# Two attentions on one core: the second scores of a turn of six heads go through a copy on VectorE, and ScalarE takes their exponential last

## The chip, the cores and the metric

The kernel runs on one core of a Trainium2 chip. The metric is the device time of one execution in microseconds, as the median of several runs. The engines are named as in the profile: PE (TensorE; its weight loads have the row PEld), DVE (VectorE), ACT (ScalarE), POOL (GpSimd) and SP (SyncE, whose queue issues nearly all DMAs of the part that matters here).

## What is computed

The reference has two attentions over 2048 tokens of width 576, each with 32 heads of 18 columns; their outputs stand side by side. A is plain attention with one key and one value head for all 32 query heads. B has keys and values for each head, works in four segments of 512 tokens, is causal within a segment and mixes in a memory of the segments before.

```python
# A
scores = einsum("bhqd,bkd->bhqk", q, k) * Dh ** -0.5
o = einsum("bhqk,bkd->bhqd", softmax(scores), v)          # then @ wo
# B, for segment s of 4
logits = einsum("bhqd,bhkd->bhqk", qs, ks) * Dh ** -0.5 + mask
a_dot = einsum("bhqk,bhkd->bhqd", softmax(logits), vs)
num, den = phi(qs) @ M, phi(qs) @ z + 1e-6
o = g * num / den + (1 - g) * a_dot                       # then @ wo
M, z = M + phi(ks).T @ vs, z + phi(ks).sum()
```

## The kernel before

The first stage (up to about 330 us) projects queries, keys and values and stores them in HBM. The second stage, in which the change lies, is the attention. Its scores are made transposed: 128 keys on the partitions, 512 queries in the free dimension. A block is four heads of one chunk of 512 queries: 32 blocks of A (4 chunks of 8) with 16 key tiles each, and 32 blocks of B (4 segments of 8) with 3 steps each. The list `after` says behind which A blocks the pairs of B blocks come.

An item is a step of a block with one pair of heads. `scores` makes the two heads of an item with two matmuls (a step of B with two key tiles: four) that run in two halves of the array's rows, into a tile E of two PSUM banks (line 726 for A, 734 for B). ScalarE takes the exponential of the whole tile E into an SBUF tile P (L727, L737); in B, POOL then clears what lies above the diagonal (L741). There are three tiles E (six banks) and nine tiles P. The other two banks are O, in which `products` sums the four heads of a block (L761, columns of 32, so that four heads run side by side), and F, in which the output projection is made in pieces (`out_part`, L648).

The order of PE, ScalarE and VectorE is written out by hand as turns. A turn holds three items, so six heads; where the 32 items of an A block do not divide by three, one turn has two. A turn emits the scores of its three items with their exponentials, then one piece of an output projection if there is one (`run_fill(1)`, four matmuls), then the products of the turn that lies two back. The first item of a turn takes the tile E that the first item of the last turn had, and so on.

```python
for k in range(len(turns) + 2):
    for n, pr in turns[k] if k < len(turns) else []:
        scores(its[n], pr)
    run_fill(1)
    for n, hf in prods[k - 2] if k > 1 else []:
        ...
```

Behind the products of the last blocks of a chunk comes a chain of small steps, put off by turns in the list `later`: VectorE copies O to SBUF (oe, L770) and SP stores it; `sums` loads the softmax sums back (sm), `inverses` takes their reciprocals on VectorE (L609) and stores them; `load_heads` loads the heads (oc) and the reciprocals spread over the columns (rb; in B behind the first segment also the memory's part, nb and another rb); `weigh` multiplies them on VectorE (L634 to L642); then the pieces of the chunk's projection are ready, and each twelfth of it is copied out of F by VectorE (osb, L672) and stored by SP. At most one such step is emitted a turn, and only in turns whose products are A's. The pieces that are left when the scores end are made in a tail, and behind them the projection of the last chunk, which goes into all eight banks.

B's values come from HBM for a whole segment at a time (`load_vseg`, two buffers). `prefetch` loads the stacks of queries and keys one stack (eight heads) ahead.

Of the kernel before, what the change touches and what calls it, by code (L numbers as in the profile page):

```python
# [7 lines left out]
F32 = mybir.dt.float32  # L8
# [3 lines left out]
AF = mybir.ActivationFunctionType  # L12
ALU = mybir.AluOpType
# [5 lines left out]
S, D, H, DH = 2048, 576, 32, 18  # L19
NSEG, L = 4, 512  # L20
C = 512
NCH = S // C
NKT = S // 128
# [3 lines left out]
SCALE = DH ** -0.5  # L27
# [5 lines left out]
KR = 56  # L33
VW = DH + 1
# [3 lines left out]
HALF = (0, 64)  # L38
# [3 lines left out]
BKEYS = [[(0, 0)], [(1, 0)], [(2, 0), (3, 256)]]  # L42
# [17 lines left out]
def attention_pair_kernel(ctx, tc, a_xT, a_w, a_wo, b_xT, b_w, b_wo, b_beta, ident_d, hmask_d, bmask_d, cmask_d, sel_d, zmask_d, selx_d, sely_d, out):  # L60
    nc = tc.nc
# [552 lines left out]

    def load_heads(ab, c, t):
        o_d, r_d = (oA, rA) if ab == "A" else (oB, rB)
        tiles = [pa.tile([128, C], F32, name=n, bufs=4) for n in ("oc", "rb")]
        if ab == "B" and c > 0:
            tiles += [pa.tile([128, C], F32, name=n, bufs=4) for n in ("nb", "rb2")]
        lo, n, R = H0[t], HT[t], RT[t]  # L620
        nc.sync.dma_start(tiles[0][:R], o_d[c][lo : lo + n, 1:VW, :])
        nc.sync.dma_start(tiles[1][:R], r_d[c][lo : lo + n, None, :].to_broadcast([n, DH, C]))
        if ab == "B" and c > 0:
            nc.sync.dma_start(tiles[2][:R], numB[c][DH * lo : DH * lo + R])
            nc.sync.dma_start(tiles[3][:R], rdB[c][lo : lo + n, None, :].to_broadcast([n, DH, C]))
        return tiles

    def weigh(ab, c, t, tiles):

        R = RT[t]  # L630
        o = parts[ab, c][:R, t]
        oc, rb = (x[:R] for x in tiles[:2])
        if ab == "A":
            nc.vector.tensor_tensor(o, oc, rb, op=ALU.mult)  # L634
            return
        if len(tiles) == 2:
            nc.vector.scalar_tensor_tensor(o, oc, omg[:R, t : t + 1], rb, op0=ALU.mult, op1=ALU.mult)
            return
        nc.vector.scalar_tensor_tensor(oc, oc, omg[:R, t : t + 1], rb, op0=ALU.mult, op1=ALU.mult)
        nb, rb2 = (x[:R] for x in tiles[2:])  # L640
        nc.vector.tensor_tensor(nb, nb, rb2, op=ALU.mult)
        nc.vector.tensor_tensor(o, oc, nb, op=ALU.add)  # L642

    def out_part(ab, c, i, t, dst, c0, n, start, stop):

# [69 lines left out]
    def scores(it, pr):  # L715
# [6 lines left out]
        state.setdefault(it, []).append(p)  # L722
        if ab == "A":
            for j, r0 in enumerate(HALF):
                rows = slice(r0, r0 + KR)
                nc.tensor.matmul(e[:, j], kstA[rows, 128 * kt : 128 * kt + 128], st[rows, h, :], start=True, stop=True)  # L726
            nc.scalar.activation(p, e, AF.Exp, scale=SCALE)  # L727
            return
        n = 512 - 128 * kt if kt < 2 else 384
        for k, c0 in BKEYS[kt]:  # L730
            ks = slice(128 * k, 128 * k + 128)
            for j, r0 in enumerate(HALF):
                rows = slice(r0, r0 + KR)
                nc.tensor.matmul(  # L734
                    e[:, j, c0 : c0 + 512 - 128 * k], st[rows, 4 + h, ks], st[rows, h, 128 * k :], start=True, stop=True
                )
        nc.scalar.activation(p[:, :, :n], e[:, :, :n], AF.Exp, scale=SCALE)  # L737

        m = len(BKEYS[kt])
        diag = p.rearrange("p a (b t) -> p a b t", t=256)[:, :, 0:m, 0:128]  # L740
        nc.gpsimd.affine_select(  # L741
            diag, diag, pattern=[[0, 2], [0, m], [1, 128]], base=0, channel_multiplier=-1, compare_op=ALU.is_ge, fill=0.0
        )

    acc = {}

    def products(it, hf):

        ab, c, hg, kt = it
        if kt == hf == 0:  # L750
            acc[0] = psO.tile([128, C], F32, name="O")
        o = acc[0]
        ps_ = state.pop(it) if hf else state[it]
        last = NKT - 1 if ab == "A" else 2
        k, p0, q0, n = (kt, 256 * hf, 256 * hf, 256) if ab == "A" else BHALF[kt][hf]
        for j in range(4):
            if ab == "A":
# [3 lines left out]
            nc.tensor.matmul(  # L761
                o[32 * j : 32 * j + 32, q0 : q0 + n],
                v,
                ps_[j // 2][:, j % 2, p0 : p0 + n],
                start=kt == hf == 0,
                stop=kt == last and hf == 1,
            )
        if kt == last and hf:
            osb = pa.tile([128, C], F32, name="oe", bufs=2)
            nc.vector.tensor_copy(osb, o)  # L770
# [13 lines left out]
    prefetch("B", 1)  # L784
    load_vseg(0)
    FILL = 60
    later, weighed, loaded = [], {}, [0]

    def at(k, ready, step):
        later.append((k, ready, step))  # L790
        later.sort(key=lambda e: e[0])

    def due(k, n=1):

        for e in [e for e in later if e[0] <= k]:
            if n and e[1]():
                later.remove(e)
                e[2](k)
                n -= 1

    def finish(k, ab, c, hg):

        ts = range(4) if hg == 6 else range(4, 5)
        lo, hi = (0, 28) if hg == 6 else (28, 32)
        box = {}
        weighed.setdefault((ab, c), 0)
        last = (ab, c) == blocks[-1][:2]
        d1, d2, step = (2, 3, 1) if last else (2, 5, 1) if ab == "A" or c == 0 else (2, 7, 2)

        def begin(k):  # L810
            loaded[0] += len(ts)
            box[0] = sums(ab, c, lo, hi)
            at(k + d1, lambda: True, inv)

        def inv(k):
            inverses(ab, c, lo, hi, box[0])
            for t in ts:
                box[t, t] = load_heads(ab, c, t)
                at(
                    k + d2 + step * (t - ts[0]),  # L820
                    lambda: (ab, c) in parts or len(parts) - filled[0] // FILL < 2,
                    lambda k, t=t: heads(k, t),
                )

        def heads(k, t):
            if (ab, c) not in parts:
                parts[ab, c] = pa.tile([128, 5, C], F32, name="o", bufs=2)
            weigh(ab, c, t, box[t, t])
            loaded[0] -= 1
            weighed[ab, c] += 1  # L830
            if weighed[ab, c] == 5 and not last:
                at(k + 1, lambda: True, lambda k: fill.append(out_proj(ab, c)))

        at(k + (0 if last else 1), lambda: loaded[0] + len(ts) <= 4, begin)

    def split(n, cut):

# [5 lines left out]
    with tc.manual_schedule(engines={ENG.PE, ENG.Activation, ENG.DVE}):  # L843
# [8 lines left out]
                at_ = split(len(items), cut)  # L852
                out_ += [items[a:z] for a, z in zip(at_, at_[1:])]
        for k in range(len(turns) + 2):
            for n, pr in turns[k] if k < len(turns) else []:
                scores(its[n], pr)
            run_fill(1)
            for n, hf in prods[k - 2] if k > 1 else []:
                it = its[n]
                hg = products(it, hf)  # L860
                if hg in (6, 7):
                    finish(k, it[0], it[1], hg)
            if k > 1 and its[prods[k - 2][-1][0]][0] == "A":
                due(k)
            for n, pr in turns[k] if k < len(turns) else []:
                it = its[n]
                ab = it[0]
                if pr == 0:
                    prefetch(ab, keys[ab].index((ab, it[1], it[2] // 2)) + 2)
                    if it in (("A", 0, 0, 4), ("A", 0, 2, 4)):  # L870
                        load_wo(*(("A", a_wo) if it[2] == 0 else ("B", b_wo)))
                    if ab == "B" and it[2] == 4 and it[3] == 0 and it[1] + 1 < NSEG:
                        load_vseg(it[1] + 1)

        ab, c = blocks[-1][:2]
        while fill:
# [80 lines left out]
```

## Time and profile before

| | us |
|---|---|
| median of 3 runs | 1524.0 (1523.32 to 1524.51) |
| the profiled execution, its own time | 1525.33 |
| its span (first to last instruction) | 1523.6 |
| PE busy in the span | 1474.2 |
| ScalarE busy in the span | 1234.7 |
| VectorE busy in the span | 316.6 |
| first exponential of the attention starts at | 330.9 |
| last exponential ends at | 1467.3 |

The granted PE clock is 0.992 over the span and 1.00 in every stretch of the attention from 380 us to 1480 us. A line of a view by groups reads: line of the kernel, engine, operation, tile written and tiles read, shape, count, then the busy time of the group and the mean duration of one, then the idle time of the engine ahead of the group and what ended it. A line of the timeline reads: start, length, engine, line, operation, tiles, shape and count (neighbours of one kind are merged), then in brackets the idle time of the engine before it and what ended it.

### The profile page before, as it was taken

The numbers are of one execution on the slowest core, as the hardware profiler recorded it, in microseconds if no ns is written. First come the engines' busy times: TensorE is split into PE (matmuls) and PEld (weight loads), VectorE is DVE, ScalarE is ACT, GpSimd is POOL, SyncE is SP. The second block draws the span as 40 slices with busy tenths as digits, with TensorE's granted clock in tenths as the row PEclk, the third lists the DMA queues.
The fourth block names the chain that finished last, engine by engine and source line by source line (L and its number), as shares of the span: only waits on it lengthen the run. The fifth ranks groups of instructions, "written<-read, shape, count | busy, mean of one in ns | idle before, by whom it ended". The sixth has DMA issues, their size and how long they took to land.

```text
span 1523.6 us, 40356 instructions
## 1 busy us (share of the span) xinstructions
PE 1474.2 (97%) x17540; PEld 840.1 (55%) x17540; DVE 316.6 (21%) x607; ACT 1234.7 (81%) x1456; POOL 119.3 (8%) x221
## 2 busy tenths in 40 slices
PE   8989999999999999999999999999999999999998
PEld 5668878754444555545555454555554444444454
DVE  6564673530011001211000001112012100100011
ACT  3333334259999999999999999999999999999950
POOL 0030000002121111001001010111100000000000
PEclk9989999999999999999999999999999999999999
DMA  6775643456464243432332213342322111010011
GB/s 196 232 234 175 188 153 128 139 169 185 128 187 134 59 135 108 152 101 71 95 101 69 89 51 103 105 144 73 102 90 77 53 41 47 27 52 16 32 64 60
DMA packets 87983, 166.29 MB, mean 109 GB/s; under 512 B 12480, under 2 KB 21242, under 8 KB 87626
## 3 DMA queue, kind: packets, MB, share of 16 engines
q1 hardware_dynamic: 81510, 157.82, 33.4%
q10 hardware_dynamic: 6291, 5.85, 1.2%
q8 instruction: 138, 2.26, 0.6%
q14 instruction: 44, 0.35, 0.1%
HBM read 96.15 MB, written 67.49 MB: 107 GB/s over the span
## 4 chain that ended last, share of the span: by engine, by line
PE 64%; ACT 7%; DMA 3%; issue 3%; SPq 1%; DVE 0%; ACTq 0%; DVEq 0%
PE O L761 28%; PE E L726 21%; PE F L648 12%; ACT P L727 5%; PE E L734 3%; ACT P L737 2%; DMA stB<-qB 1%; PE E L648 1%; DMA woA<-a_wo 1%; DMA stB<-shB 0%; SPq L577 0%; DMA stA<-qA 0%; DVE osb L672 0%; DMA oB<-oe 0%; DMA stB<-ones_d 0%
## 5 line engine op out<-in xcount | busy, mean ns | idle before, releaser
L727 ACT ACTIVATE P<-E 128x1024 f32<-128x1024 f32 x1024 | 958.7, 1040 | 16.5 <-PE E L726 4.7
L761 PE MATMUL O<-P,VA 128*32 128x256 f32 x8192 | 509.3, 380 | 0.1
L726 PE MATMUL E<-stA,kstA 56*128 56x512 f32 x1920 | 367.7, 457 | 9.9 <-ACT P L727 7.4
L761 PEld LDWEIGHTS O<-P,VA 128*32 128x32 f32 x8192 | 261.4, 110 | 148.0 <-issue 10.1
L726 PEld LDWEIGHTS E<-stA,kstA 56*128 56x128 f32 x1920 | 154.4, 184 | 244.5 <-ACT P L727 239.1
L737 ACT ACTIVATE P<-E 128x768 f32<-128x768 f32 (+1 forms) x192 | 155.2, 898 | 8.4 <-PE E L734 7.2
L672 DVE COPY osb<-F 128x192 f32<-128x192 f32 x84 | 30.0, 358 | 594.9 <-PE F L648 594.9
L741 POOL TENSOR_SCALAR_AFFINE_SELECT P<-P 128x256 f32<-128x256 f32 (+1 forms) x192 | 94.6, 493 | 666.6 <-ACT P L737 663.4
L770 DVE COPY oe<-O 128x512 f32<-128x512 f32 x64 | 44.3, 692 | 405.5 <-PE O L761 348.8
L648 PE MATMUL F<-woB,o 126*32 126x192 f32 (+1 forms) x1920 | 127.0, 338 | 0.0
L648 PE MATMUL F<-woA,o 126*32 126x192 f32 (+2 forms) x1480 | 88.7, 337 | 6.1 <-DVE osb L672 6.1
L101 ACT CAST qp<-pj 126x512 fp32r<-126x512 f32 (+1 forms) x56 | 32.6, 584 | 64.7 <-DVE kmB L351 48.4
L761 PE MATMUL O<-P,vseg 128*32 128x256 f32 (+2 forms) x1536 | 81.5, 344 | 0.3 <-POOL P L741 0.2
L199 PE MATMUL pj<-xh,wBh 128*126 128x512 f32 x180 | 74.6, 419 | 3.4 <-DVE xh L171 3.4
L199 PE MATMUL pj<-xh,wBl 128*126 128x512 f32 x180 | 73.2, 406 | 0.0
L734 PE MATMUL E<-stB 56*128 56x256 f32 (+3 forms) x512 | 66.8, 354 | 5.6 <-ACT P L737 3.9
L648 PEld LDWEIGHTS F<-woB,o 126*32 126x32 f32 (+1 forms) x1920 | 38.5, 108 | 58.6 <-issue 53.8
L734 PEld LDWEIGHTS E<-stB 56*128 56x128 f32 x512 | 40.5, 184 | 40.7 <-ACT P L737 16.4
L761 PEld LDWEIGHTS O<-P,vseg 128*32 128x32 f32 x1536 | 48.2, 109 | 25.5 <-issue 2.7
L199 PE MATMUL pj<-xl,wBh 128*126 128x512 f32 x144 | 60.3, 419 | 0.0
L648 PEld LDWEIGHTS F<-woA,o 126*32 126x32 f32 (+1 forms) x1480 | 34.6, 108 | 43.6 <-issue 26.6
L102 DVE TENSOR_TENSOR qp<-pj,qp 126x512 fp32r<-126x512 f32 (+1 forms) x56 | 38.2, 686 | 55.7 <-ACT qp L101 55.5
(124 smaller groups left out, 998.7 us busy)
## 6 DMA issues: line engine op xcount, KB each, us to landing
stB<-kB SPq DMA_DIRECT2D x96, 144.0 KB
stB<-qB SPq DMA_DIRECT2D x32, 288.0 KB
stA<-qA SPq DMA_DIRECT2D x30, 288.0 KB
oA<-oe SPq DMA_DIRECT2D x32, 256.0 KB
oB<-oe SPq DMA_DIRECT2D x32, 256.0 KB
qA<-qp SPq DMA_DIRECT2D x16, 504.0 KB
kB<-qp SPq DMA_DIRECT2D x16, 504.0 KB
qB<-qp SPq DMA_DIRECT2D x16, 504.0 KB
```

What stands on the lines that cost most here:

```text
L101: nc.scalar.copy(qp[:R, 0, :n], src)
L102: nc.vector.tensor_tensor(qp[:R, 1, :n], src, qp[:R, 0, :n].bitcast(F32), op=ALU.subtract)
L199: nc.tensor.matmul(dst, w[:, c0 : c0 + M], x, start=i == 0, stop=i == len(ops) - 1)
L648: nc.tensor.matmul(dst[32 * j : 32 * j + 32], parts[ab, c][: RT[t], t, r0 : r0 + 32], wo[ab][: RT[t], t, c0 : c0 + n], start=start, stop=stop,
L672: nc.vector.tensor_copy(osb[:, cs], pf[:, :192])
L726: nc.tensor.matmul(e[:, j], kstA[rows, 128 * kt : 128 * kt + 128], st[rows, h, :], start=True, stop=True)
L727: nc.scalar.activation(p, e, AF.Exp, scale=SCALE)
L734: nc.tensor.matmul(e[:, j, c0 : c0 + 512 - 128 * k], st[rows, 4 + h, ks], st[rows, h, 128 * k :], start=True, stop=True)
L737: nc.scalar.activation(p[:, :, :n], e[:, :, :n], AF.Exp, scale=SCALE)
L741: nc.gpsimd.affine_select(diag, diag, pattern=[[0, 2], [0, m], [1, 128]], base=0, channel_multiplier=-1, compare_op=ALU.is_ge, fill=0.0)
L761: nc.tensor.matmul(o[32 * j : 32 * j + 32, q0 : q0 + n], v, ps_[j // 2][:, j % 2, p0 : p0 + n], start=kt == hf == 0, stop=kt == last and h ...
L770: nc.vector.tensor_copy(osb, o)
```

## The change

`scores` no longer takes the exponential itself but returns it as a function. For the second item of a turn of three, VectorE copies E into a new SBUF tile W (two buffers), and the exponential reads W. The turn emits the exponentials in the order first, third, second. Turns of two items keep the bank as source and their order.

Beside that, the chain of small steps is cut finer: `weigh` returns its VectorE operations one by one; `due` runs in every turn, B's too, and emits up to two steps, of which the single weighing operations cost one each; loads of heads are emitted one by one while fewer than three are loaded, and their weighing comes five turns later in all chunks but the last. To make room for W (8 KB a partition), oc, rb, nb and the second rb have three buffers instead of four, and the values of B one instead of two: the values of the next segment are loaded when the last product of a segment has been emitted. The list `after` is moved by a block in six places.

```diff
-        tiles = [pa.tile([128, C], F32, name=n, bufs=4) for n in ("oc", "rb")]
+        tiles = [pa.tile([128, C], F32, name=n, bufs=3) for n in ("oc", "rb")]
...
-    after = [0, 0, 1, 1, 2, 3, 4, 5, 8, 10, 12, 14, 16, 17, 18, 19]
+    after = [0, 0, 1, 1, 2, 3, 3, 4, 8, 9, 10, 12, 16, 17, 18, 20]
...
-        v = pa.tile([128, 4, H * VW + 13], F32, name="vseg", bufs=2)
+        v = pa.tile([128, 4, H * VW + 13], F32, name="vseg", bufs=1)
...
-            nc.scalar.activation(p, e, AF.Exp, scale=SCALE)
-            return
...
+        src = e
+        if copied:
+            src = pp.tile([128, 2, 512], F32, name="W", bufs=2)
+            nc.vector.tensor_copy(src[:, :, :n], e[:, :, :n])
+
+        def exponential():
+            nc.scalar.activation(p[:, :, :n], src[:, :, :n], AF.Exp, scale=SCALE)
...
+        return exponential
...
-    def due(k, n=1):
+    def due(k, most=2, heavy=2):
 
+        cost = 0
         for e in [e for e in later if e[0] <= k]:
-            if n and e[1]():
+            if most and cost + e[1] <= heavy and e[2]():
                 later.remove(e)
-                e[2](k)
-                n -= 1
+                e[3](k)
+                cost += e[1]
+                most -= 1
...
-        d1, d2, step = (2, 3, 1) if last else (2, 5, 1) if ab == "A" or c == 0 else (2, 7, 2)
+        d1, d2 = (2, 3) if last else (2, 5)
...
-        at(k + (0 if last else 1), lambda: loaded[0] + len(ts) <= 4, begin)
+        at(k + (0 if last else 1), 0, lambda: hg not in summing and loaded[0] < 3, begin)
...
-            for n, pr in turns[k] if k < len(turns) else []:
-                scores(its[n], pr)
+            exps = [scores(its[n], pr, i == 1 and len(turns[k]) == 3) for i, (n, pr) in enumerate(turns[k])] if k < len(turns) else []
+            for i in (0, 2, 1) if len(exps) == 3 else range(len(exps)):
+                exps[i]()
             run_fill(1)
...
-            if k > 1 and its[prods[k - 2][-1][0]][0] == "A":
-                due(k)
+                if hg == 7 and ab == "B" and c + 1 < NSEG:
+                    load_vseg(c + 1)
+            due(k)
```

More of the change, by code (lines that the diff above doesn't have):

```diff
@@ L616, in load_heads @@
         o_d, r_d = (oA, rA) if ab == "A" else (oB, rB)
-        tiles = [pa.tile([128, C], F32, name=n, bufs=4) for n in ("oc", "rb")]
+        tiles = [pa.tile([128, C], F32, name=n, bufs=3) for n in ("oc", "rb")]
         if ab == "B" and c > 0:
-            tiles += [pa.tile([128, C], F32, name=n, bufs=4) for n in ("nb", "rb2")]
+            tiles += [pa.tile([128, C], F32, name=n, bufs=3) for n in ("nb", "rb2")]
         lo, n, R = H0[t], HT[t], RT[t]
@@ L632, in weigh @@
         oc, rb = (x[:R] for x in tiles[:2])
+        v = nc.vector
         if ab == "A":
-            nc.vector.tensor_tensor(o, oc, rb, op=ALU.mult)
-            return
+            return [lambda: v.tensor_tensor(o, oc, rb, op=ALU.mult)]
         if len(tiles) == 2:
-            nc.vector.scalar_tensor_tensor(o, oc, omg[:R, t : t + 1], rb, op0=ALU.mult, op1=ALU.mult)
-            return
-        nc.vector.scalar_tensor_tensor(oc, oc, omg[:R, t : t + 1], rb, op0=ALU.mult, op1=ALU.mult)
+            return [lambda: v.scalar_tensor_tensor(o, oc, omg[:R, t : t + 1], rb, op0=ALU.mult, op1=ALU.mult)]
         nb, rb2 = (x[:R] for x in tiles[2:])
-        nc.vector.tensor_tensor(nb, nb, rb2, op=ALU.mult)
-        nc.vector.tensor_tensor(o, oc, nb, op=ALU.add)
+        return [
+            lambda: v.scalar_tensor_tensor(oc, oc, omg[:R, t : t + 1], rb, op0=ALU.mult, op1=ALU.mult),
+            lambda: v.tensor_tensor(nb, nb, rb2, op=ALU.mult),
+            lambda: v.tensor_tensor(o, oc, nb, op=ALU.add),
+        ]
     def out_part(ab, c, i, t, dst, c0, n, start, stop):
@@ L713, in load_vseg, with scores @@
         vseg[s] = v
-    def scores(it, pr):
+    def scores(it, pr, copied):
         ab, c, hg, kt = it
@@ L721, in scores @@
         p = pp.tile([128, 2, 512], F32, name="P", bufs=PBUFS)
-        state.setdefault(it, []).append(p)
+        state[it, pr] = p
+        n = 512 if ab == "A" else 512 - 128 * kt if kt < 2 else 384
         if ab == "A":
@@ L726, in scores @@
                 nc.tensor.matmul(e[:, j], kstA[rows, 128 * kt : 128 * kt + 128], st[rows, h, :], start=True, stop=True)
[L727 to L735, printed above, removed]
-                )
@@ L737, in scores @@
[L737 to L743, printed above, removed]
+        else:
+            for k, c0 in BKEYS[kt]:
+                ks = slice(128 * k, 128 * k + 128)
+                for j, r0 in enumerate(HALF):
+                    rows = slice(r0, r0 + KR)
+                    nc.tensor.matmul(
+                        e[:, j, c0 : c0 + 512 - 128 * k], st[rows, 4 + h, ks], st[rows, h, 128 * k :], start=True, stop=True
+                    )
@@ new lines, in scores @@
+        src = e
[4 more added lines that the diff above has]
+            nc.scalar.activation(p[:, :, :n], src[:, :, :n], AF.Exp, scale=SCALE)
+            if ab == "B":
+                m = len(BKEYS[kt])
+                diag = p.rearrange("p a (b t) -> p a b t", t=256)[:, :, 0:m, 0:128]
+                nc.gpsimd.affine_select(
+                    diag, diag, pattern=[[0, 2], [0, m], [1, 128]], base=0, channel_multiplier=-1, compare_op=ALU.is_ge, fill=0.0
+                )
@@ L745, in attention_pair_kernel, with products @@
+        return exponential
     acc = {}
-    def products(it, hf):
-        ab, c, hg, kt = it
-        if kt == hf == 0:
+    def products(b, m, hf):
+        ab, c, hg = b
+        if m == hf == 0:
             acc[0] = psO.tile([128, C], F32, name="O")
         o = acc[0]
-        ps_ = state.pop(it) if hf else state[it]
-        last = NKT - 1 if ab == "A" else 2
-        k, p0, q0, n = (kt, 256 * hf, 256 * hf, 256) if ab == "A" else BHALF[kt][hf]
+        last = (NKT - 1 if ab == "A" else 2) == m
@@ L756, in products @@
         for j in range(4):
+            kt = m
+            p = state[b + (kt,), j // 2]
+            k, p0, q0, n = (kt, 256 * hf, 256 * hf, 256) if ab == "A" else BHALF[kt][hf]
             if ab == "A":
@@ L763, in products @@
                 v,
-                ps_[j // 2][:, j % 2, p0 : p0 + n],
-                start=kt == hf == 0,
-                stop=kt == last and hf == 1,
+                p[:, j % 2, p0 : p0 + n],
+                start=m == hf == 0,
+                stop=last and hf == 1,
             )
-        if kt == last and hf:
+        if last and hf:
             osb = pa.tile([128, C], F32, name="oe", bufs=2)
@@ L786, in attention_pair_kernel, with at @@
     FILL = 60
-    later, weighed, loaded = [], {}, [0]
-    def at(k, ready, step):
-        later.append((k, ready, step))
+    later, weighed, loaded, summing = [], {}, [0], set()
+    def at(k, cost, ready, step):
+        later.append((k, cost, ready, step))
         later.sort(key=lambda e: e[0])
-    def due(k, n=1):
+    def due(k, most=2, heavy=2):
+        cost = 0
         for e in [e for e in later if e[0] <= k]:
-            if n and e[1]():
+            if most and cost + e[1] <= heavy and e[2]():
                 later.remove(e)
-                e[2](k)
-                n -= 1
+                e[3](k)
+                cost += e[1]
+                most -= 1
+        return cost
     def finish(k, ab, c, hg):
@@ L807, in finish, with load @@
         last = (ab, c) == blocks[-1][:2]
-        d1, d2, step = (2, 3, 1) if last else (2, 5, 1) if ab == "A" or c == 0 else (2, 7, 2)
+        d1, d2 = (2, 3) if last else (2, 5)
         def begin(k):
-            loaded[0] += len(ts)
+            summing.add(hg)
             box[0] = sums(ab, c, lo, hi)
-            at(k + d1, lambda: True, inv)
+            at(k + d1, 0, lambda: True, inv)
         def inv(k):
             inverses(ab, c, lo, hi, box[0])
+            summing.remove(hg)
             for t in ts:
[L818 to L823, printed above, removed]
+                at(k, 0, lambda: loaded[0] < 3, lambda k, t=t: load(k, t))
+        def load(k, t):
+            loaded[0] += 1
+            box[t, t] = load_heads(ab, c, t)
+            at(
+                k + d2,
+                1,
+                lambda: (ab, c) in parts or len(parts) - filled[0] // FILL < 2,
+                lambda k, t=t: heads(k, t),
+            )
         def heads(k, t):
@@ L827, in heads @@
                 parts[ab, c] = pa.tile([128, 5, C], F32, name="o", bufs=2)
-            weigh(ab, c, t, box[t, t])
+            if not isinstance(box[t, t][0], type(heads)):
+                box[t, t] = weigh(ab, c, t, box[t, t])
+            box[t, t].pop(0)()
+            if box[t, t]:
+                at(k, 1, lambda: True, lambda k: heads(k, t))
+                return
             loaded[0] -= 1
@@ L831, in heads @@
             if weighed[ab, c] == 5 and not last:
[L832 to L834 removed]
+                at(k + 1, 0, lambda: True, lambda k: fill.append(out_proj(ab, c)))
+        at(k + (0 if last else 1), 0, lambda: hg not in summing and loaded[0] < 3, begin)
     def split(n, cut):
@@ L854, in attention_pair_kernel @@
         for k in range(len(turns) + 2):
-            for n, pr in turns[k] if k < len(turns) else []:
-                scores(its[n], pr)
+            exps = [scores(its[n], pr, i == 1 and len(turns[k]) == 3) for i, (n, pr) in enumerate(turns[k])] if k < len(turns) else []
+            for i in (0, 2, 1) if len(exps) == 3 else range(len(exps)):
+                exps[i]()
             run_fill(1)
             for n, hf in prods[k - 2] if k > 1 else []:
-                it = its[n]
-                hg = products(it, hf)
+                ab, c = its[n][:2]
+                hg = products(its[n][:3], its[n][3], hf)
                 if hg in (6, 7):
-                    finish(k, it[0], it[1], hg)
-            if k > 1 and its[prods[k - 2][-1][0]][0] == "A":
-                due(k)
+                    finish(k, ab, c, hg)
+                if hg == 7 and ab == "B" and c + 1 < NSEG:
+                    load_vseg(c + 1)
+            due(k)
             for n, pr in turns[k] if k < len(turns) else []:
@@ L871, in attention_pair_kernel @@
                         load_wo(*(("A", a_wo) if it[2] == 0 else ("B", b_wo)))
-                    if ab == "B" and it[2] == 4 and it[3] == 0 and it[1] + 1 < NSEG:
-                        load_vseg(it[1] + 1)
         ab, c = blocks[-1][:2]
```

## The prediction, made before the result was known

> **What bounds the kernel now.** I read the page first (shares and slices), then the waits, then the timeline of one stretch. The slices show two stages: up to some 330 us the projections, with ScalarE at three tenths, then the attention with PE and ScalarE both at nine tenths, then a tail in which ScalarE stops.
>
> ```profile
> PE 1474.2 (97%) x17540; PEld 840.1 (55%) x17540; DVE 316.6 (21%) x607; ACT 1234.7 (81%) x1456; POOL 119.3 (8%) x221
> ...
> ACT  3333334259999999999999999999999999999950
> ```
>
> Two engines at nine tenths can each be the bound, or wait for each other too briefly for the tenths to show. The waits tell which:
>
> ```profile
> PEld E L726 <- ACT P L727: 259.9, 637, 1.4
> ```
>
> 637 times the weights of the next scores waited for an exponential to free their bank, for 259.9 us in all. VectorE is in no wait of the scores. The timeline of a stretch late in the run shows the turn (scores of six heads as three pairs, one piece of an output projection, the products of an older turn):
>
> ```profile
> 1203.76 1.11 PE L726 MATMUL E<-stA,kstA 56*128 56x512 f32 x6
> 1204.37 0.19 PEld L726 LDWEIGHTS E<-stA,kstA 56*128 56x128 f32 x2 [0.31 <-ACT P L727]
> ...
> 1204.81 0.53 PE L648 MATMUL F<-woB,o 126*32 126x192 f32 x8
> ...
> 1205.16 1.48 PE L761 MATMUL O<-P,VA 128*32 128x256 f32 x24
> ...
> 1206.57 1.20 PE L726 MATMUL E<-stA,kstA 56*128 56x512 f32 x6
> ...
> 1207.27 0.19 PEld L726 LDWEIGHTS E<-stA,kstA 56*128 56x128 f32 x2 [0.41 <-ACT P L727]
> ...
> 1209.46 1.12 PE L726 MATMUL E<-stA,kstA 56*128 56x512 f32 x6
> ```
>
> The reader is to see that the third pair's weights (the "x2") wait for ScalarE in each turn, and that the distance of the scores alternates: 2.81, then 2.89 us. Taken apart into single instructions the trace gives a loop of two halves. PE's half: from the end of the third exponential to the start of the third pair 0.05, to its end 0.50, projection piece, products and the next first pair 2.18 (always 2.183 to 2.186 in 101 turns), to the next first exponential 0.10: 2.85 us in round numbers. ScalarE's half: starts 0.903 and 0.920 apart, the third exponential 1.03 long: 2.85. Each half waits for the other, so two turns cost 5.70 and one 2.85.
>
> I laid all 1216 exponentials out by turn. 258 turns of three A pairs with A products and a piece take 735.7 us, 2.851 each. Without a piece they take 2.742 (31 turns, leaving out one of 4.56 at the start). 28 A turns beside the smaller B products take 2.719 (minimum 2.708, three times the 0.903): there ScalarE alone sets the pace. PE's own pace is 2.18 + 2 x 0.226 (end of the first pair to end of the second, when nothing waits) = 2.635. So of 2.851 us some 0.13 belong to the loop and to neither engine.
>
> **What the change removes.** In a three-pair turn the second pair's bank is freed by VectorE, and ScalarE takes the third pair second. PE's wait for the third bank thus ends one exponential (0.92 us) earlier, PE's half of the loop no longer ends on time with ScalarE's, and ScalarE always has scores waiting. What is late next is ScalarE itself: three exponentials, one of them from SBUF. The instruction order confirms that it does what it says: 384 copies on VectorE, and on ScalarE two exponentials from a bank, then one from the copy.
>
> **The exponential from SBUF.** The attention of before has none; the first stage has ScalarE operations of 512 columns from both memories:
>
> ```profile
> 234.56 0.59 ACT L335 ACTIVATE aq<-pj 72x512 bf16<-72x512 f32 x1 [0.82 <-PE tr L329]
> 235.05 0.58 ACT L299 ACTIVATE ph_e<-pj 126x512 f32<-126x512 f32 x1
> 235.53 0.39 ACT L389 COPY vch<-pj 128x288 f32<-128x288 f32 x1
> 235.81 0.65 ACT L300 ACTIVATE ph_e<-ph_e 126x512 f32<-126x512 f32 x1
> ...
> 236.34 0.17 ACT L391 COPY kn<-pj 128x18 f32<-128x18 f32 x1
> ```
>
> From a PSUM bank (pj) the next instruction starts 0.48 to 0.49 after, from SBUF (ph_e) 0.53. I take 0.05 more for each exponential from the copy, between 0 (the latency hides behind the neighbour) and 0.10 (its successor pays too). [...]
>
> **The copies.** Line L770 copies 512 columns out of PSUM in 692 ns, line L672 192 in 358:
>
> ```profile
> L770 DVE COPY oe<-O 128x512 f32<-128x512 f32 x64 | 44.3, 692 | 405.5 <-PE O L761 348.8 <-POOL P L741 42.3 <-DMA oB<-oe 10.3
> L672 DVE COPY osb<-F 128x192 f32<-128x192 f32 x84 | 30.0, 358 | 594.9 <-PE F L648 594.9
> ```
>
> That is 1.04 ns a column, so 1024 cost 1.23 us and 768 (32 of the 384) 0.96: 463 us in all, on an engine that was busy 132 us of the last 1184. Beside a turn of 2.77 they are hidden. The copy starts when the second pair is done, some 0.78 us after the last turn's first exponential ended, and ends 2.0 after it; its exponential is due 3.5 after it. So the cover is 1.5 us, and a VectorE held longer than that stalls ScalarE one for one.
>
> **The sum**, against the profiled execution (span 1523.6, its own time 1525.3):
> - A turns of three pairs: ScalarE's 2.719 + 0.05 = 2.769. 258 x (2.851 - 2.769) = 21.2 saved; 31 x 0.027 and 28 x 0.05 lost, 2.2. Net **-19.0** (with 0 for SBUF -35, with 0.10 -3).
> - A turns of two pairs (32, 2.00 us; ScalarE alone 1.82) keep the old order: some 0.18 is saved there, but the turn after again waits for a last exponential and gives it back. **0** (-5 to +3).
> - B turns (64, 166 us): the first of a block is at ScalarE's pace already in 18 cases (2.51), the second (2.60 with a piece, 2.27 without, ScalarE's three 768s 2.1) hangs on PE's five score pairs. 44 have a piece; 0.1 each, less the surcharge: **-3** (-8 to +3).
> - The new weighing in B turns starts projections sooner: by the instruction order 64 pieces stand behind the last scores and were 73. In the tail five pieces take 2.315 us (below), so 9 x 0.463 = **-4.2**. The 9 moved pieces cost PE 0.44 each in turns that ScalarE sets: nothing.
> - VectorE's holds: **+2** (below).
>
> ```profile
> 1474.83 1.83 PE L648 MATMUL F<-woA,o 126*32 126x192 f32 x40 [0.84 <-DVE osb L672]
> 1476.73 0.36 DVE L672 COPY osb<-F 128x192 f32<-128x192 f32 x1 [1.96 <-PE F L648]
> 1477.14 1.46 PEld L648 LDWEIGHTS F<-woA,o 126*32 126x32 f32 x40 [0.85 <-DVE osb L672]
> ```
>
> Smaller edits: one values buffer instead of two, loaded (1216 KB) when the last product of a segment is done; in the new order the next B block comes 10 turns later (28 us), so it is hidden. It goes ahead of the small load for the last heads' sums, whose reciprocal stands two turns on: at 180 GB/s, the rate of the busiest attention slices, 7 us against 5.5 and the cover; this is the +2. Three buffers for oc, rb instead of four: loads start five turns (14 us) ahead of their weighing, hidden. A heavy turn (copy 1.23, oe 0.69, two weighings 1.4) takes VectorE 3.3 and is caught up in the next.
>
> In sum 24.2 us less: 1501.1, and as the median of the runs is 1.3 below the profiled execution, **1500 us**.
>
> **Rivals.**
> 1. *VectorE held by transfers* (slower). All that VectorE waits for now stands ahead of a copy. Its waits for DMA in the attention add up to 58.8 us in 11 (10.30, 10.21, 6.26, 5.93, 5.32 the longest). If each held a copy, less 1.5 of cover, 42 us return: 1540. It decides from 27 us of holds. Against: laid against the turns, only one of them (0.70 us) began after its next turn's first exponential; to the rest VectorE had come early. For: new queue order. 0.14.
> 2. *ScalarE is at its floor already* (slower): the 2.85 would be its own, the surcharge comes on top, 1525 + 19 - 4 = 1540, 1539 as a median. The turns at 2.719 speak against it. [...] 0.05.
> 3. *PE is the bound*: if a pair costs 0.335 us (start to start of the first two) and not 0.226, PE's turn is 2.85 and only the tail is gained: 1520. The regular 0.226 speaks against it. 0.17, half of it within the noise.
> 4. *The SBUF read costs nothing*: 16 us more saved in A turns, some in B: 1481. All rows speak against it. 0.14.
> My forecast (1489 to 1513): 0.50.
>
> About 0.2% (3 us) is what a measurement can tell from no change. Faster: 0.50 + 0.14 + half of 0.17 = 0.73; same 0.08; slower 0.14 + 0.05 = 0.19. The range from 1480 takes in rivals 3 and 4 and ends at 1527, leaving out the slower ones.
>
> **What would show it.** Right: A turns with a piece near 2.77 us without alternation; first and third exponentials 0.90 to 0.92 from start to start, 0.95 to 0.97 after the one from W; hardly a wait of E's weights for ScalarE; copies near 1.23 us. Wrong: waits of ScalarE for W (rival 1), turns at 2.85 with PE without gaps (3) or with ScalarE without gaps (2).

## The result and the profile after

The changed kernel takes 1508.7 us (median of 4 runs, 1505.4 to 1513.0), the kernel before beside it 1524.3 (4 runs, 1523.3 to 1525.5): a ratio of 0.990 [0.9885, 0.9917], 15.5 us less where 24 were predicted. The profiled execution, from which all durations here come, was the fastest of the four: its own time is 1505.42 us, its span 1503.4, its granted PE clock 0.993. Against the profiled execution of before that is 19.9 us less.

First the page: busy times, ScalarE's slices, and the groups of the exponentials and of the new copy.

```profile
PE 1439.7 (96%) x17540; PEld 838.8 (56%) x17540; DVE 770.7 (51%) x991; ACT 1224.3 (81%) x1456; POOL 120.6 (8%) x221
...
ACT  3333334259989999999999999999999999999950
...
L743 ACT ACTIVATE P<-E 128x1024 f32<-128x1024 f32 (+1 forms) x832 | 803.6, 1066 | 10.6 <-PE E L734 6.7
L740 DVE COPY W<-E 128x1024 f32<-128x1024 f32 (+1 forms) x384 | 460.9, 1201 | 473.2 <-PE E L728 376.2
L743 ACT ACTIVATE P<-W 128x1024 f32<-128x1024 f32 (+1 forms) x384 | 426.1, 1110 | 12.3 <-DVE W L740 12.3
```

The shares of PE and ScalarE have hardly moved (97 to 96%, 81 to 81%): the page's first parts would not tell that the kernel is faster. VectorE has 454 us more to do; its 384 copies take 1.20 us each, 461 in all. New is the end of the last line: ScalarE was idle for 12.3 us ahead of an exponential from W, and the copy ended all of it.

Then the timeline of three turns late in the run:

```profile
1251.77 0.96 PE L728 MATMUL E<-stA,kstA 56*128 56x512 f32 x6
1252.62 1.23 DVE L740 COPY W<-E 128x1024 f32<-128x1024 f32 x1 [1.43 <-PE E L728]
1252.63 1.98 ACT L743 ACTIVATE P<-E 128x1024 f32<-128x1024 f32 x2
...
1254.43 0.96 PE L728 MATMUL E<-stA,kstA 56*128 56x512 f32 x6
1254.44 1.12 ACT L743 ACTIVATE P<-W 128x1024 f32<-128x1024 f32 x1
...
1255.38 2.00 ACT L743 ACTIVATE P<-E 128x1024 f32<-128x1024 f32 x2
...
1257.07 0.96 PE L728 MATMUL E<-stA,kstA 56*128 56x512 f32 x6
1257.19 1.14 ACT L743 ACTIVATE P<-W 128x1024 f32<-128x1024 f32 x1
```

The six scores of a turn ("x6") now take 0.96 us, where they took 1.11 to 1.20 with the third pair's wait in them: in these turns no pair is held up by ScalarE, and PE's turns are 2.66 and 2.64 apart. ScalarE runs without a gap, 2.75 us a turn (1252.63 to 1255.38): starts 0.903 apart, and 0.948 behind the exponential from W (medians over the three-pair A turns). The loop of two halves is gone.

One sign did not come as forecast. The waits still have 425 entries of E's weights behind ScalarE:

```profile
PEld E L728 <- ACT P L743: 159.3, 425, 1.3
```

They are of two kinds. 189 of them, all ahead of a turn's first pair, start well behind any end of an exponential; the same 0.41 stands before the weights of the turns above with "issue" as its releaser. That is the ordinary distance to the weight load before, put down to the last semaphore. The other 236, of which 166 are third pairs, start within 0.07 us of the end of an exponential and are real waits, as here:

```profile
607.37 2.00 ACT L743 ACTIVATE P<-E 128x1024 f32<-128x1024 f32 x2
...
608.84 1.07 PE L728 MATMUL E<-stA,kstA 56*128 56x512 f32 x6
...
609.41 0.19 PEld L728 LDWEIGHTS E<-stA,kstA 56*128 56x128 f32 x2 [0.28 <-ACT P L743]
```

The third pair's weights start 0.04 behind the end of ScalarE's second exponential (609.37), which frees their bank, and the six scores take 1.07 us. Of 288 three-pair A turns behind another, 109 have a third pair that starts within 0.06 us of that end; before, behind the third exponential, 275 had. PE is ahead of ScalarE here, so the wait costs no time (ScalarE's next exponential starts at 610.12, 0.95 behind the one from W at 609.17), but it bounds how far ahead PE can get (behind 1000 us the copy starts, by the medians of a block's turns, at most 0.41 ahead of its turn's first exponential; e7).

All 1216 exponentials laid out by turn, with the long turns (over 0.35 us above the median of their kind, where a wait explains them) taken apart, give the difference between the two profiled executions:

| | predicted | measured |
|---|---|---|
| three-pair A turns | -19.0 | -16.8 |
| two-pair A turns (32) | 0 | -5.5 |
| B turns (64) | -3 | -5.2 |
| tail | -4.2 | -3.9 |
| long turns | +2 | +14.9 |
| first stage, its code untouched | 0 | -3.8 |
| sum, by the spans | -24.2 | -20.2 |

(The rows are rounded, so that they add up to 0.1 more than the spans give.) The 3.8 us of the first stage are not the change's: the start of the attention lies between 325.7 and 330.9 us in the profiled executions of this document, all with the same code ahead of it.

The long turns are nine A turns, 14.3 us above their medians, and two B turns that wait for a stack of queries and keys (2.9), less 2.3 of such turns in before. In three of the nine (5.88 us) VectorE waits for the softmax sums, in three and the turn behind one of them (6.57) for what a weighing needs, in one (0.81) for a buffer oe; in the ninth (1.06) two weighings stand ahead of the copy, with no wait for a transfer over 0.4 us. The longest, in the timeline of all engines (SPq is SP's queue as it issues DMAs):

```profile
609.23 0.66 SPq L621 DMA_DIRECT2D oc<-oB  x1
609.68 1.23 DVE L740 COPY W<-E 128x1024 f32<-128x1024 f32 x1 [0.51 <-PE E L728]
...
610.82 0.68 DVE L641 TENSOR_TENSOR nb<-nb,rb 126x512 f32<-126x512 f32 x1
...
612.88 2.03 ACT L743 ACTIVATE P<-E 128x1024 f32<-128x1024 f32 x2
...
615.71 0.75 DVE L640 SCALAR_TENSOR_TENSOR oc<-oc,omg,rb 72x512 f32<-72x512 f32 x1 [4.21 <-DMA oc<-oB]
616.38 1.21 DVE L740 COPY W<-E 128x1024 f32<-128x1024 f32 x1
...
617.69 1.06 ACT L743 ACTIVATE P<-W 128x1024 f32<-128x1024 f32 x1 [2.78 <-DVE W L740]
```

VectorE comes to a weighing at 611.5 and waits 4.21 us for its heads. The copy of the turn stands behind it, starts at 616.38, and ScalarE, which is through with the two exponentials from the banks, waits 2.78 us for W. That turn takes 5.77 us. The weighing was emitted five turns or more behind its load; SP, whose queue had waited for older transfers (this load itself, 1.0 us, for one of queries that was issued at 599.17), issued the load only at 609.23, 2.3 us ahead of VectorE's arrival, and it landed 6.5 us after its issue.

### The profile page after: what moved, and what is told of

The parts are those of the page before. It is cut to its first block, busy times and chain, and to the rows that moved or that the text cites. A ratio compares the mean times of both kernels' runs of the same rounds, so it can differ in the third digit from the quotient of the medians.

```text
span 1503.4 us, 40869 instructions
## 1 busy us (share of the span) xinstructions
PE 1439.7 (96%) x17540; PEld 838.8 (56%) x17540; DVE 770.7 (51%) x991; ACT 1224.3 (81%) x1456; POOL 120.6 (8%) x221
## 4 chain that ended last, share of the span: by engine, by line
PE 59%; DMA 8%; ACT 6%; SPq 2%; issue 2%; DVE 1%; ACTq 0%; DVEq 0%
PE O L772 27%; PE E L728 18%; PE F L649 11%; ACT P L743 6%; PE E L734 3%; DMA stB<-qB 2%; DMA oB<-oe 1%; DMA rB<-sm 1%; PE E L649 1%; DMA stA<-qA 1%; DMA rb<-rB 1%; DMA woA<-a_wo 1%; SPq L577 1%; DVE W L740 0%; DMA woB<-b_wo 0%
## 5 line engine op out<-in xcount | busy, mean ns | idle before, releaser
L743 ACT ACTIVATE P<-E 128x1024 f32<-128x1024 f32 (+1 forms) x832 | 803.6, 1066 | 10.6 <-PE E L734 6.7
L740 DVE COPY W<-E 128x1024 f32<-128x1024 f32 (+1 forms) x384 | 460.9, 1201 | 473.2 <-PE E L728 376.2
L743 ACT ACTIVATE P<-W 128x1024 f32<-128x1024 f32 (+1 forms) x384 | 426.1, 1110 | 12.3 <-DVE W L740 12.3
L728 PE MATMUL E<-stA,kstA 56*128 56x512 f32 x1920 | 337.1, 443 | 18.1 <-ACT P L743 8.9
L772 PEld LDWEIGHTS O<-P,VA 128*32 128x32 f32 x8192 | 262.8, 110 | 151.0 <-issue 10.7
L102 DVE TENSOR_TENSOR qp<-pj,qp 126x512 fp32r<-126x512 f32 (+1 forms) x56 | 38.2, 686 | 55.6 <-ACT qp L101 55.4
```

The lines of the kernel that those rows point to most:

```text
L102: nc.vector.tensor_tensor(qp[:R, 1, :n], src, qp[:R, 0, :n].bitcast(F32), op=ALU.subtract)
L740: nc.vector.tensor_copy(src[:, :, :n], e[:, :, :n])
L743: nc.scalar.activation(p[:, :, :n], src[:, :, :n], AF.Exp, scale=SCALE)
L772: nc.tensor.matmul(o[32 * j : 32 * j + 32, q0 : q0 + n], v, p[:, j % 2, p0 : p0 + n], start=m == hf == 0, stop=last and hf == 1,)
```

## The experiments

Theory: the gain is the loop's (copy and order together), the finer steps bring nothing of it, and what is missing went into VectorE's holds. Rivals: the steps bring the gain; the order alone or the copy alone brings it; the 8 us that are missing belong to the copy itself.

**e1, the steps alone.** No copy, exponentials in the old order, all else as in the changed kernel.

```diff
-            exps = [scores(its[n], pr, i == 1 and len(turns[k]) == 3) for i, (n, pr) in enumerate(turns[k])] if k < len(turns) else []
-            for i in (0, 2, 1) if len(exps) == 3 else range(len(exps)):
+            exps = [scores(its[n], pr, False) for i, (n, pr) in enumerate(turns[k])] if k < len(turns) else []
+            for i in range(len(exps)):
```

> All of the change but the copy and the order: the second exponential reads its bank, in the order first, second, third. Theory (the copy and the order together break the loop between PE and ScalarE; the other edits only shorten the tail): three-pair A turns with a piece at 2.85 us as before, the tail some 4 us shorter, 1520 us (1515 to 1525). Rival (the finer steps and the moved B blocks bring the gain): near the 1509 of the changed kernel.

Measured 1529.3 (1528.2 to 1530.3), ratio 1.004 [1.0025, 1.0059]. So the steps bring no gain; they cost 6.7 us where a small one was expected. The turns are those of before. One turn, at 473.8 us, takes 11.45 us, 8.7 above the median, which is more than the loss; the timeline has it:

```profile
476.98 0.35 SPq L783 DMA_DIRECT2D oA<-oe  x1
...
481.01 0.69 DVE L781 COPY oe<-O 128x512 f32<-128x512 f32 x1 [10.63 <-DMA oA<-oe]
...
481.76 2.79 PE L772 MATMUL O<-P,VA 128*32 128x256 f32 x24 [6.76 <-DVE oe L781]
```

VectorE waits for one of the two buffers oe, whose store SP issues only at 476.98, behind loads of a stack (eight, from 471.03 to 476.62); O is not emptied, and PE waits 6.76 us. This hold needs no copy: the first products of the next block wait for O.

**e2, the order alone.** The changed kernel without the copy: ScalarE takes first, third, second, all from the banks.

```diff
-            exps = [scores(its[n], pr, i == 1 and len(turns[k]) == 3) for i, (n, pr) in enumerate(turns[k])] if k < len(turns) else []
+            exps = [scores(its[n], pr, False) for i, (n, pr) in enumerate(turns[k])] if k < len(turns) else []
```

> The changed kernel without the copy: order first, third, second, all from their banks. Theory: PE writes the second pair ahead of the third, and the second bank is now freed by the last exponential, so PE's half of the loop grows by one pair (0.23 us) to 3.06 against 2.85 for ScalarE's: turns near 2.95, 1548 us (1535 to 1560). Rival (freeing the third bank earlier is enough): at or under 1512.

Measured 1528.7 (1524.0 to 1529.4), ratio 1.003 [1.0015, 1.0044], like e1. The expectation was wrong: the order costs nothing. (The hold of e1 is here too, a turn of 10.40 us at 476.6.)

```profile
1246.22 1.48 PE L772 MATMUL O<-P,VA 128*32 128x256 f32 x24
...
1247.62 0.30 PEld L728 LDWEIGHTS E<-stA,kstA 56*128 56x128 f32 x4 [0.41 <-ACT P L743]
1247.63 1.15 PE L728 MATMUL E<-stA,kstA 56*128 56x512 f32 x6
1248.27 0.19 PEld L728 LDWEIGHTS E<-stA,kstA 56*128 56x128 f32 x2 [0.35 <-ACT P L743]
```

The first two pairs ("x4") go through and the third waits, as in before: its weights start at 1248.27, 0.05 behind the end of the turn's last exponential (1248.22). I had kept the banks fixed to the pairs; then the second pair would have had to wait for that last exponential, and it doesn't. The trace reads as a new tile E taking the bank that is released next, so that the second pair of a turn gets the bank of the exponential that comes second. With every tile freed by ScalarE, the order only renames the banks here, and the time is that of e1 (1528.7 and 1529.3).

**e3, the copy alone.** The changed kernel with the exponentials in the order first, second, third.

```diff
-            for i in (0, 2, 1) if len(exps) == 3 else range(len(exps)):
+            for i in range(len(exps)):
```

> The changed kernel with the copy but the order first, second, third. Theory: the third bank is freed last as before (PE's half 2.85), and the second exponential has to wait for its copy: second pair done 0.23 us after the first, copy 1.23 and two hand-overs, so it starts 1.48 after the first exponential and not 0.90; ScalarE's half 3.43, two turns 6.3, a turn 3.1: 1600 us (1565 to 1625). Rival (a bank freed by VectorE is enough, the order does nothing): near 1509.

Measured 1644.9 (1644.4 to 1646.7), ratio 1.080 [1.0783, 1.0819]: the direction is right, the loss 45 us larger and outside what was expected. Against the profiled execution of before the A turns of three pairs take 110 us more (3.18 in the mean) and the B turns 17. The group of the exponentials from W:

```profile
L743 ACT ACTIVATE P<-W 128x1024 f32<-128x1024 f32 (+1 forms) x384 | 399.2, 1040 | 98.5 <-DVE W L740 90.7
```

ScalarE waits 98.5 us for W, and the plain A turn with a piece takes 3.05 us (median). The copy has one exponential of cover here and two in the changed kernel; the third pair again hangs on ScalarE's last exponential (E's weights wait 285.5 us for ScalarE in all, 159.3 in the changed kernel). So neither half of the change brings anything by itself.

**e4, copy and order on the old steps.** The kernel before, with the copy, the order and, to make room for W, one values buffer; the old chain of steps, the old list `after`, four buffers of oc and rb.

```diff
-        v = pa.tile([128, 4, H * VW + 13], F32, name="vseg", bufs=2)
+        v = pa.tile([128, 4, H * VW + 13], F32, name="vseg", bufs=1)
...
+        if copied:
+            src = pp.tile([128, 2, 512], F32, name="W", bufs=2)
+            nc.vector.tensor_copy(src[:, :, :n], e[:, :, :n])
...
+            for i in (0, 2, 1) if len(exps) == 3 else range(len(exps)):
+                exps[i]()
```

> The kernel before with the copy and the new order, and one values buffer to make room (loaded behind the last product of a segment); old steps, old place of the B blocks, four buffers for oc and rb. Theory: A turns at 2.754 us as in the changed kernel; the old steps put each wait for a transfer on VectorE later than the transfer in all but one case, so few holds; tail 9 pieces (4 us) longer: 1497 us (1490 to 1506). If holds come with any step: 1510 to 1520. Rival (the steps and the moved blocks bring the gain): 1520 or more.

Measured 1504.9 (1502.4 to 1507.4), ratio 0.988 [0.9866, 0.9901], inside what was expected. Copy and order alone bring the whole gain; the finer steps, with the change of buffers and of the list, add nothing that can be seen (the two ratios' intervals overlap). They save 3.1 us of tail (55.6 to 52.5) and give it back in holds: ScalarE's idle time ahead of W is 6.0 us here, 12.3 there.

```profile
L742 ACT ACTIVATE P<-W 128x1024 f32<-128x1024 f32 (+1 forms) x384 | 426.7, 1111 | 6.0 <-DVE W L739 5.7
```

**e5, the steps later.** The changed kernel with more turns between a load and what needs it.

```diff
-        d1, d2 = (2, 3) if last else (2, 5)
+        d1, d2 = (2, 3) if last else (4, 8)
```

> The changed kernel with its small steps put off: the reciprocals four turns behind their loads instead of two, the weighing eight turns behind its loads instead of five (not in the last chunk). Nothing on VectorE then stands ahead of a copy while its transfer is under way. Theory (the holds of VectorE by transfers eat the part of the gain that is missing): the long turns between 435 and 620 us shrink to 2.8, but those of the copies out of O (waiting for a store) and of the last chunk stay; some 11 us of holds gone, 8 more pieces in the tail (3.7 us): 1501 us (1495 to 1505). Rival (the long turns come from PE's own transfers or from the clock): long turns stay, 1509 to 1514.

Measured 1497.8 (1497.4 to 1498.7), ratio 0.983 [0.9814, 0.9847]: as expected, by the medians 10.9 us under the changed kernel.

```profile
L743 ACT ACTIVATE P<-W 128x1024 f32<-128x1024 f32 (+1 forms) x384 | 429.9, 1119 | 0.3
```

ScalarE's wait for W is 0.3 us in place of 12.3, and no A turn is long any more; the plain turn stays at 2.754. The turns that were expected to stay long, those of the copies out of O and of the last chunk, whose steps this edit leaves alone, are within 0.31 of the plain turn too, and no run shows why. The tail is 2.4 us longer (72 pieces are left for it in place of 64). So the holds are what was missing: with the same copies and later steps they vanish. By the two profiled executions the gain is 7.7 us, as the changed kernel was profiled in its fastest run.

**e6, the copy in turns of two as well.** In the changed kernel a turn of two frees both banks by ScalarE.

```diff
-            exps = [scores(its[n], pr, i == 1 and len(turns[k]) == 3) for i, (n, pr) in enumerate(turns[k])] if k < len(turns) else []
+            exps = [scores(its[n], pr, i == 1) for i, (n, pr) in enumerate(turns[k])] if k < len(turns) else []
```

> The changed kernel with the copy in the turns of two items too (the second of two, whose exponential is the last anyway). Theory (the turn behind a turn of two, 3.05 us, waits for a bank that the last exponential of the turn of two frees): turns of two 1.85 us (1.807 and the 0.044 of the SBUF read), the turn behind 2.754 or, in B, 2.56: 32 x 0.04 lost, 31 x 0.3 saved, 1501 us (1498 to 1504). Rival (the turn behind is long for another reason, its products or the weights of the new block): 1508 to 1511.

Measured 1496.1 (1493.2 to 1498.0), ratio 0.982 [0.9797, 0.9833]. The mechanism is as expected: the A turn behind a turn of two takes 2.754 (3.057 in the changed kernel), the turn of two itself 1.97 in the mean (1.81; 1.85 was expected). The size isn't: by the medians 12.7 us are gained where 4.7 to 10.7 were expected, while the attention of the two profiled executions differs by 6.9. Of the other 5.8, 4.0 are that the changed kernel was profiled 3.3 under its median and this one 0.7 over it, and 1.4 lie in the first stage, which the edit doesn't touch; so about 6.9 is what the edit shows.

**e7, holds of known length.** In six A turns of three late in the run the copy is made two, three or four times. Nothing is computed otherwise.

```diff
-            nc.vector.tensor_copy(src[:, :, :n], e[:, :, :n])
+            for _ in range(copied):
+                nc.vector.tensor_copy(src[:, :, :n], e[:, :, :n])
...
+        more = {333: 2, 377: 2, 344: 3, 388: 3, 366: 4, 399: 4}
```

> The changed kernel with the copy made two, three and four times over in two late A turns each (turns 333 and 377, 344 and 388, 366 and 399), so that VectorE is held 1.22, 2.45 and 3.67 us longer with nothing else changed. Theory (the cover of a copy is 1.5 us, a longer hold stalls ScalarE one for one): those turns 2.754 + 0, + 0.95, + 2.2 us, 6.3 us in sum. If the cover were none: + 1.2, 2.4, 3.7, 14.6 in sum. If the third bank and not the copy were what ScalarE waits for: + 0 in all.

One run: 1518.2. The turn with one copy too many takes 3.41 us, 0.66 over the 2.754; with two 4.65 and 4.67, 1.9 over; with three 5.93 and 5.91, and with the turns behind them 3.86 and 3.71 over. The theory's 0, 0.95 and 2.2 are wrong, and in the turn itself (3.41, 4.65, 5.93) each copy beyond the first too many costs about its length, 1.22 us. The first leaves 1.22 - 0.66 = 0.56 us of cover. All six turns are the sixth of their block, so this is the cover there and not everywhere. A turn with three too many:

```profile
1316.44 6.13 DVE L741 COPY W<-E 128x1024 f32<-128x1024 f32 x5 [1.42 <-PE E L728]
1316.57 2.00 ACT L744 ACTIVATE P<-E 128x1024 f32<-128x1024 f32 x2
...
1321.50 0.50 PE L728 MATMUL E<-stA,kstA 56*128 56x512 f32 x2 [2.37 <-DVE W L741]
1321.54 1.06 ACT L744 ACTIVATE P<-W 128x1024 f32<-128x1024 f32 x1 [2.97 <-DVE W L741]
```

The copy begins as the turn's first exponential does (1316.44 and 1316.57). PE waits for the same copies, 2.37 us, since the bank they read is its next. Over the changed kernel behind 1000 us the copies start 0.12 us ahead of the turn's first exponential (median; from 0.43 ahead to 0.30 behind it in 8 of 10 turns), and end 0.71 before their own exponential could begin (0.28 to 1.01). The forecast's cover of 1.5 us would have put the start 0.92 ahead (an exponential from W is due 1.81 behind the first one's start, less 1.5, less 1.23 for the copy); behind 1000 us no copy starts more than 0.52 ahead. The start moves within a block: by the medians 0.30 behind in the block's second turn, then 0.1 earlier each turn, 0.13 ahead in the sixth, and 0.41 and 0.40 ahead in the last two turns of three, where it stops, since the third pair has to wait for ScalarE's second exponential.

**e8, all three.** The copy in turns of two, three buffers for oe (the wait of e1), and the steps somewhat later.

```diff
-            osb = pa.tile([128, C], F32, name="oe", bufs=2)
+            osb = pa.tile([128, C], F32, name="oe", bufs=3)
...
-        d1, d2 = (2, 3) if last else (2, 5)
+        d1, d2 = (2, 3) if last else (4, 6)
...
-            exps = [scores(its[n], pr, i == 1 and len(turns[k]) == 3) for i, (n, pr) in enumerate(turns[k])] if k < len(turns) else []
+            exps = [scores(its[n], pr, i == 1) for i, (n, pr) in enumerate(turns[k])] if k < len(turns) else []
```

> The changed kernel with the copy in the turns of two, the reciprocals four and the weighing six turns behind their loads, and three buffers for oe. Theory: 9 us from the turns behind a turn of two, 11 to 14 from the holds, 4 more pieces in the tail (1.9 us): 1489 us (1484 to 1496). If holds and turns of two are not what is missing: 1505 or more.

Measured 1491.7 (1487.9 to 1493.7), ratio 0.979 [0.9777, 0.9811], as expected: by the median the fastest kernel here, 17 us under the changed one and 32 under the one before it. ScalarE still waits 2.6 us for W.

## Why the prediction was right, and where it wasn't

The sign and the mechanism were right: 1508.7 lies in the range, 8.7 above the forecast. By its steps:

- **The loop.** Right. Taken apart it gave 2.85 us as two halves that wait for each other, with 0.13 in neither engine; the changed kernel runs at ScalarE's pace, and where PE waits in a plain turn, it is ahead of ScalarE. (The terms given for PE's half add up to 2.83, not 2.85; nothing else hangs on that.) Rivals 2 (ScalarE at its floor) and 3 (PE the bound) would have left 2.85; the turns are 2.754. e3 shows that both parts of the edit are needed, e2 that the order by itself is nothing.
- **The exponential from SBUF.** Right: 0.05 was taken, 0.045 measured (0.948 against 0.903). The turn is 2 x 0.903 + 0.948 = 2.754, 0.015 under the forecast's 2.769; over some 300 turns that is 4.5 us better. Rival 4 (no surcharge) falls.
- **Turns of two.** Right in kind: 0.20 is saved in the turn (2.007 to 1.807) and the turn behind takes 0.28 more (2.774 to 3.057). The A turns in all, long ones left out, gave 22.3 us where 19.0 stood.
- **B turns and tail.** -5.2 and -3.9, against -3 and -4.2. The -3 doesn't follow from its own terms: 44 x 0.1 less 0.05 for each of 64 is 1.2.
- **VectorE's holds.** This is the term that was mis-sized: +2 was forecast, and nine A turns cost 14.3 us. The one hold that the +2 stood for came (the turn at 442.5, where VectorE waits 5.70 us for the sums while the values load is under way) and cost 2.65; the others were put at nothing. Two steps under the term failed. "So the cover is 1.5 us": it is about 0.56 in the sixth turn of a block (e7), and mostly the copy ends 0.3 to 1.0 us before it is due. The reckoning let PE run on as soon as ScalarE's first exponential was done. But the third pair's bank is freed by ScalarE's second exponential, and that stops PE about half a microsecond short of that lead (the copy starts 0.41 ahead in place of 0.92). And PE's turn of 2.65 us gains only 0.1 on ScalarE's 2.75, so that a lead, once lost in a turn of two, in a B block or in a hold, comes back over about seven turns (from 0.30 behind to 0.41 ahead at 0.1 a turn). And "loads start five turns (14 us) ahead of their weighing, hidden": five turns lie between the emissions, but SP's queue issued the load of the longest hold 2.3 us before VectorE needed it. "A VectorE held longer than that stalls ScalarE one for one" was right within the turn, with the shorter cover; the two longest holds of e7 cost 0.5 to 0.7 more in the turns behind.
- **Rival 1** was the right one to fear, with the right price per hold. It decides from 27 us of holds; VectorE's came to 14.3 behind the cover. In the forecast's sum, the same rival at a third of its size belonged into the forecast itself.
- **Luck.** Against the 12.9 us of long turns that were not forecast stand 5.5 in the turns of two, which pay for what the turns behind them lose, 2.2 in the B turns, and 3.8 in the first stage, which has nothing to do with the change. That the profiled executions differ by 20.2 where 24.2 stood is in part these 3.8.

What stays open: why the four runs of the changed kernel spread over 7.5 us (the two slower ones have a mean granted clock of 0.989 and 0.987 against 0.993) where e5's spread over 1.3, and the stack that comes late at 364 us in the changed kernel and, alike, in e4 to e6 and e8, for which PE waits 2 us or more (the B turns at 364 and 369; in e1 and e2 1.7 and 1.4 us).

## What to carry to other kernels

Two engines that both stood at nine tenths in the attention's slices still waited for each other once a turn: 0.13 us of 2.851 belonged to neither. The single starts showed it, the shares didn't, and a third engine that freed one buffer between them removed it (2.754 a turn), since the order let the copy have two exponentials of cover (with one, in e3, the kernel took 1.080 of the time before). The copy, put into VectorE's queue, then made the waits ahead of it its own: 4.21 us of waiting for one load there held ScalarE for 2.78. So count the waits of all that stands ahead of it, and reckon its cover from the pace of the new loop and from the buffer that holds its producer back (it came to about 0.56 us in the sixth turn of a block), not from the lead that the first free buffer would allow (1.5). The distance between a load and its use has to be read where the queue issues the load: SP's queue issued the load of the longest hold 2.3 us ahead of VectorE's arrival, where the program left five turns or more (five are some 14 us).

## What the runs showed of the hardware that I had not expected

- The same copy of 1.2 us costs 8% of the kernel's time where one exponential covers it (e3) and saves 1% where two do.
- An exponential of 1024 columns from SBUF delays its successor by 0.045 us against PSUM, and nothing more: the plain turn of 2 x 0.903 + 0.948 us is 2.754 in the changed kernel and in e5 alike.
- A hold in VectorE's queue reaches PE by two ways: through the bank that the copy frees (2.37 us in e7, 2.19 in the longest hold of the changed kernel) and through the sums in O (e1, 6.76 us of PE's time behind one store).
